# Fewer, wider TensorE products, four more staging tiles and four zero stores under way in a decode attention and GEGLU backward kernel

## The chip, the cores and the metric

The kernel runs on one core of a Trainium2 chip. The metric is device microseconds (us) for one execution of the whole program.

## The reference

The program computes a layer's forward output and its gradients with `jax.vjp`, for one new token in each of 4 batch rows (D = 512, 32 query heads, 8 key/value heads, Dh = 128, cache length 4096, F = 1792, all bfloat16):

```python
def _A_ref(x, k_cache, v_cache, wq, wo):           # attention over the last W positions
    W = min(4096, max(256, Sk // 4))               # 1024 of 4096
    q = (x @ wq).reshape(B, Sq, Hq, Dh).transpose(0, 2, 1, 3)
    k = repeat(k_cache[:, :, Sk - W:, :], 4, axis=1)
    v = repeat(v_cache[:, :, Sk - W:, :], 4, axis=1)
    p = softmax(einsum("bhqd,bhkd->bhqk", q, k) * Dh ** -0.5)
    o = einsum("bhqk,bhkd->bhqd", p, v)
    return o.transpose(0, 2, 1, 3).reshape(B, Sq, Hq * Dh) @ wo
def _B_ref(x, w_gate, w_up, w_down):
    return (gelu(x @ w_gate) * (x @ w_up)) @ w_down
xn = layernorm(x)
f = x + _A_ref(xn, k_cache, v_cache, wq, wo) + _B_ref(xn, w_gate, w_up, w_down)
out, vjp = jax.vjp(f, ...);  return (out, *vjp(grad_out))
```

Nine outputs result: the layer's output and the gradients to x, the two caches (33.6 MB each), wq, wo, w_gate, w_up and w_down. Positions before the window have a gradient of zero, so three quarters of each cache gradient are zeros that must be written.

## The kernel before

The kernel has four stages.

*FFN.* The rows are replicated so that row `Q*b + i` (Q = 32) of x and grad_out belongs to batch row b. `h_ps` holds the two hidden products, with four column groups of TensorE side by side; `dwd`, `dwu` and `dwg` are outer products that pass through PSUM banks, are copied into a staging tile `stg` ([128, 4096] bfloat16; the pool `stage` has 4) and stored. The gradient to the layer norm's output is summed in `dxf_ps` over 112 products of 128 columns.

*Preparation of attention.* `q_ps` gets the query, heads along its free dimension, from 128 products (32 heads by 4 chunks) that take 128x128 blocks of `wq_sb` as weights and 4 columns of `xnT` as the moving operand. ACT scales it into `qs`, DVE copies that into `qs2`; `spread_rows(0, get_q)` makes from these D3q, a form with 32x32 blocks turned for the scores, and `qm`, the rows that the gradient to K needs. Then eight 32x32 transposes of `wo_sb` on DVE feed the 32 products `do_ps`, from which `spread_rows(1, get_d)` makes D3d and `dm`. `rows[k]` has a copy for each of two heads of a quadrant.

*Attention*, a loop over the 4 batch rows. `scores(0, b)` and `scores(1, b)` give S and dP in the form [128, 256]: partition (quadrant c, j-octet a, row r), with 8 DVE transposes of K or V each. `softmax` gives `P_b`. `spread(P_b)` (4 DVE multiplications by `amask`) makes `spr`, the weights of `dvdk`; `turned` makes `pT`, positions on partitions, from `P_b` by 32 products with the selectors `selp`; `odq` multiplies `pT` by V (or K) in 32 products of 256 columns, one column group per quadrant, and picks the right one of two heads with masks `om` by one ACT step and one DVE step into `odt`. `dvdk` has 32 products per call (K = 32 rows, 256 columns) into 16 `kv_ps` banks, whose copies by `evac` fill two `stg` tiles; each is stored by `result`. The k = 1 half does the same for dS, with `rows[0]`, giving the gradient to K.

*The end.* The output, the gradient to x (`dxq_ps`, 128 products of 128 columns), then `dwo` and `dwq`, 8 `stg` tiles of 8 banks each.

TensorE, VectorE, ScalarE and GpSimd run their instructions in an order that the tile framework's scheduler works out from the program; the order on SyncE (SP) is the program's (`manual_schedule`). SP issues all loads and the 32 zero stores: `zeros(n, after)` takes the next n of the list, each 1.5 MB from `ztile`, and makes each wait until the `deep`-th one before it has landed; with `after` it waits also for a compute instruction. GpSimd (POOL) issues all result stores. `evac(out, in_, n)` copies a PSUM bank to SBUF on ACT or DVE, whichever has less work by a running estimate.

Lines that the prediction follows: 117 (`mm`, all matmuls), 88 and 89 (`evac` on ACT and DVE), 93 (`t32`, transposes), 106 (`store`), 512 (`spread`), 598 (`odq`'s DVE step).

Of the kernel before, what the change touches and what calls it, by code (L numbers as in the profile page):

```python
# [8 lines left out]
ACT = mybir.ActivationFunctionType  # L9
ALU = mybir.AluOpType  # L10
# [8 lines left out]
def kernel(  # L19
# [148 lines left out]
    def mask(name, n, in_):  # L168
# [9 lines left out]
    hm = mask("hm", Q, ident_f[:].rearrange("p (h d) -> p h d", d=4))  # L178
    omt = const.tile([P, NQ, 2], FP32, name="omt")
    TT(out=omt[:], in0=gmask[:].rearrange("p (c g) -> p c g", g=2), in1=bm[:].unsqueeze(2).broadcast_to([P, NQ, 2]),  # L180
       op=ALU.mult)
    om = mask("om", 2, omt[:].rearrange("p c g -> p g c"))
    oms = const.tile([P, 2], FP32, name="oms")
    TS(out=oms[:], in0=om[:], scalar1=scale, scalar2=None, op0=ALU.mult)
    gmask_b = const.tile([P, G], BF16, name="gmask_b")
    nc.vector.tensor_copy(out=gmask_b[:], in_=gmask[:])
# [4 lines left out]
    rs2_f = rs2[:].rearrange("p c a r -> p (c a r)")  # L191
    selp = const.tile([P, 4, NQ, 8], BF16, name="selp")
    for a in range(4):
        TS(out=selp[:, a], in0=rs2[:, :, 0, :], scalar1=amask[:, a:a + 1], scalar2=None, op0=ALU.mult)

# [31 lines left out]
    fo = const.tile([P, D], FP32, name="fo")  # L227
    dxf = const.tile([P, P], FP32, name="dxf")

# [24 lines left out]

    def zeros(n, after=None, deep=3):

        for _ in range(n):
            og, b, g = ztodo.pop(0)
            z = store(nc.sync, og[b, g:g + ZG, 0:K0, :].rearrange("g (m j) d -> m g (j d)", m=ZP), zsrc, "zeros",
                      ["rest"])  # L260
            if len(zdone) >= deep:
                behind(z.ins, zdone[-deep].ins)
            if after is not None:
                behind(z.ins, after.ins)
            zdone.append(z)


    if True:
# [81 lines left out]

        dxf_ps = bank("dxf_ps", "S", (P, P))
        nc.vector.memset(dxf_ps[:], 0.0)
        nm = 0
        for wi, (wsb, dh, og) in enumerate(((wu_sb, dhu, out_7), (wg_sb, dhg, out_6))):
# [13 lines left out]
            for ch in range(4):  # L368
                sc = scratch()
                n7 = FPB // 4  # L370
                t32(sc[:, 0:n7 * P].rearrange("p (k c n) -> p c k n", k=n7, c=C),
                    pairs(wsb[:])[:, :, ch * n7 * Q:(ch + 1) * n7 * Q], 896)
                sb = sc[:, 0:n7 * P].bitcast(BF16).rearrange("p (k n r) -> p k r n", k=n7, r=2)
                for k in range(n7):
                    for r in range(2):
                        c = nm % 4
                        mm(dxf_ps[Q * c:Q * c + 4 * B, :], dhs[:, ch * n7 + k, r, :], sb[:, k, r, :], nm < 4,
                           nm >= 4 * FPB - 4, (0, Q * c))
                        nm += 1
            dwg_v = og.rearrange("(p h c) f -> h p (c f)", h=2, c=2)  # L380
# [12 lines left out]
    with tc.tile_pool(name="mid", bufs=1, reuse_waits="tile") as mid:  # L393
# [4 lines left out]
        with tc.tile_pool(name="att", bufs=1, reuse_waits="tile") as att:  # L398
# [171 lines left out]
            def dvdk(k, b, sp, r_):  # L570

                og = (out_3, out_2)[k]
                stg = [stg_tile() for _ in range(2)]
                sv = [s_[:].rearrange("p (g j d) -> p j g d", g=4, j=J) for s_ in stg]
                for j in range(0, J, 2):
                    ps = [bank("kv_ps", "w", (P, 2, 2, Dh)) for _ in range(NQ)]
                    for u in range(2):
                        for c, q in enumerate(quad):
                            mm(ps[c][:, u].rearrange("p g d -> p (g d)"), sp[q, j + u].rearrange("p a m -> p (a m)"),
                               r_[q, b].rearrange("p g d -> p (g d)"), pos=(Q * c, 0))  # L580
                    for c in range(NQ):
                        evac(sv[c // 2][:, j:j + 2, (c % 2) * 2:(c % 2) * 2 + 2, :], ps[c][:], 512)
                for hf in range(2):
                    result(og[b, hf * 4:(hf + 1) * 4, K0:Sk, :].rearrange("g (m j) d -> m g (j d)", j=J),
                           stg[hf][:].rearrange("p (g e) -> p g e", g=4))

            def odq(k, b, pT):

                ps = bank("od_ps", "x", (P, 2, Dh))
                src = (v_t, k_t)[k][b]  # L590
                for j in range(J):
                    for c, q in enumerate(quad):
                        mm(ps[q].rearrange("p g d -> p (g d)"), pT[:, j, :], src[:, 2 * c:2 * c + 2, j, :],
                           j == 0, j == J - 1, (0, Q * c))
# [3 lines left out]
                done = STT(out=t_[:], in0=ps[:, 1, :], scalar=mk[:, 1:2], in1=t_[:], op0=ALU.mult, op1=ALU.add)  # L598
                if k == 0:
# [33 lines left out]
            for b in range(B):  # L633
# [6 lines left out]
                if b == B - 1:  # L640
                    zeros(3, p_done)
                    turn_wq()
                    dP = scores(1, b)
                pT = turned(P_b, 0)
                o_done = odq(0, b, pT)
# [3 lines left out]
                else:  # L649
                    zeros(2, o_done)  # L650
                dvdk(0, b, spread(P_b, 0), rows[1])
                dS_b = softmax_d(P_f, dP)
                dST = turned(dS_b, 1)
                o_done = odq(1, b, dST)
# [3 lines left out]
                elif b == B - 1:  # L658
                    zeros(2, o_done)
                dvdk(1, b, spread(dS_b, 1), rows[0])  # L660

        with tc.tile_pool(name="end", bufs=1, reuse_waits="tile") as end:
# [28 lines left out]

            dxq_ps = bank("dxq_ps", "dP", (P, P))
            nc.vector.memset(dxq_ps[:], 0.0)
            nm = 0
            for hc in range(8):
                for k in range(8):
                    for r in range(2):
                        c = nm % 4
                        mm(dxq_ps[Q * c:Q * c + 4 * B, :], dqs[:, hc * 4 + k // 2, k % 2, r, :],
                           wqT[hc].bitcast(BF16).rearrange("p c k (n r) -> p k r c n", r=2)[:, k, r], nm < 4,  # L700
                           nm >= 124, (0, Q * c))
                        nm += 1
# [3 lines left out]
            s_d = fin("s_d", (P, P))  # L706
            TT(out=s_d[:], in0=dxq_ps[:], in1=dxf[:], op=ALU.add)
            dn_ps = bank("dn_ps", "x", (B, 4, C, Q))
            for nb in range(4):
                mm(dn_ps[:, nb].rearrange("b c n -> b (c n)"), rsum_f[:, nb * B:(nb + 1) * B], s_d[:])  # L710
            dn = fin("dn")
# [39 lines left out]
            for c in range(C):  # L751
                stg = stg_tile()
                for u in range(2):
# [36 lines left out]
```

## Time and profile before

| | before |
|---|---|
| median of 3 runs | 281.53 us (280.95 to 282.53) |
| profiled execution | 283.22 us |
| its span | 281.5 us |
| mean granted TensorE clock | 0.595 |
| PE / PEld busy | 179.4 us (64%), 1733 products / 73.2 us |
| DVE / ACT / POOL busy | 167.6 us (60%) / 122.7 us (44%) / 50.0 us (18%) |
| DMA | 111.97 MB, mean 398 GB/s |
| read from and written to HBM | 30.68 MB and 81.01 MB |
| zero stores: 32 of 1.5 MB, issue to landing (median) | 20.6 us |
| 1 MB stores from `stg`: 24, issue to landing (median) | 15.4 us |

The span is the time from the first to the last event of the profile; the difference of 1.7 us to the profiled execution's time lies around it. "Busy" is time in which an engine works on an instruction; engines overlap. PE's products are recorded after pairing, so the page counts fewer of them than the program has. The page's 40 slices are 7.04 us each. The queue q1 holds SP's transfers, q0 POOL's, q8 the fetches of TensorE's instructions.

### The profile page before, as it was taken

To read this page: it belongs to the slowest core of one execution; us is meant where nothing else is said; L and a number is where in the kernel's file an instruction comes from. 1 tells how busy PE (TensorE), PEld (TensorE's weight loads), DVE (VectorE), ACT (ScalarE), POOL (GpSimd) and SP (SyncE) were. 2 spreads that over 40 slices of the span, in tenths; PEclk is the share of its full clock that TensorE was granted. 3 is DMA by queue.
4 is the path that set the end of the run, shared out by engine and by line. 5 is a ranking of instruction groups with operands and counts; after the bars stand their busy time and mean duration, and the time that the engine had idled before them with its cause. 6 is when DMAs were issued, how large, how long until landed. Compare 5 with 4: busy or idle time off the path is not lost.

```text
span 281.5 us, 4422 instructions
## 1 busy us (share of the span) xinstructions
PE 179.4 (64%) x1733; PEld 73.2 (26%) x1735; DVE 167.6 (60%) x310; ACT 122.7 (44%) x248; POOL 50.0 (18%) x121
## 2 busy tenths in 40 slices
PE   1157998878248778497774877504779996504470
PEld 0022452322122532225322243102236351000110
DVE  7879659888943437424484086996433439514470
ACT  3243775610129348292461823500851944413470
POOL 8500100294330402204020020200020020100010
PEclk9985955559755755555555575555555956555555
DMA  7999989999999999999999999999899999999773
GB/s 275 429 452 444 377 356 423 426 422 405 429 403 427 422 407 414 418 414 428 415 402 422 404 406 424 414 395 426 363 412 400 419 402 406 416 418 415 319 306 156
DMA packets 20340, 111.97 MB, mean 398 GB/s; under 512 B 1360, under 2 KB 1376, under 8 KB 14688
## 3 DMA queue, kind: packets, MB, share of 16 engines
q1 hardware_dynamic: 13944, 81.02, 70.5%
q0 software_dynamic: 6368, 30.67, 26.9%
q8 instruction: 13, 0.21, 0.3%
q14 instruction: 7, 0.06, 0.0%
q10 hardware_dynamic: 8, 0.00, 0.0%
HBM read 30.68 MB, written 81.01 MB: 397 GB/s over the span
## 4 chain that ended last, share of the span: by engine, by line
PE 21%; issue 20%; DMA 14%; DVE 12%; ACT 4%; POOL 1%; POOLq 0%; ACTq 0%
DMA out_dram<-stg 14%; PE kv_ps L117 11%; DVE scr L93 5%; PE od_ps L117 3%; ACT stg L88 2%; DVE stg L89 2%; DVE spr L512 2%; PE sc_ps L117 2%; PE ok_ps L117 1%; PE dwq_ps L117 1%; POOL out_dram L106 1%; PE es_ps L117 1%; PE nm_ps L117 1%; ACT E_f L544 1%; PE dqr_ps L117 1%
## 5 line engine op out<-in xcount | busy, mean ns | idle before, releaser
L88 ACT CAST stg<-kv_ps 128x512 bf16<-128x512 f32 x118 | 60.0, 650 | 5.7 <-PE kv_ps L117 5.6
L106 POOL DMA_DIRECT2D out_dram<-stg x30 | 19.7, 657 | 209.9 <-ACT stg L88 147.7
L117 PE MATMUL sc_ps<-scr,bd 128*32 128x256 bf16 x256 | 19.0, 389 | 24.2 <-DVE scr L93 24.2
L93 DVE STREAM_TRANSPOSE scr<-va 128x1024 uint32<-128x1024 uint32 x16 | 18.8, 1220 | 21.9 <-PE od_ps L117 21.6
L117 PE MATMUL kv_ps<-dm,spr 32*128 32x256 bf16 x128 | 26.3, 393 | 4.7 <-ACT stg L88 2.6
L117 PE MATMUL kv_ps<-qm,spr 32*128 32x256 bf16 x128 | 24.3, 372 | 3.9 <-ACT stg L88 2.4
L117 PEld LDWEIGHTS <-spr 32*128 32x128 bf16 x256 | 11.6, 101 | 43.0 <-issue 37.2
L117 PE MATMUL dwo_ps<-dy_b,oSP 32*128 32x512 bf16 x32 | 10.1, 549 | 12.9 <-ACT stg L88 11.9
L117 PEld LDWEIGHTS <-bd 128*32 128x32 bf16 x256 | 9.2, 117 | 33.0 <-issue 31.5
L88 ACT CAST stg<-dwo_ps 128x512 bf16<-128x512 f32 x18 | 10.0, 593 | 17.2 <-PE dwo_ps L117 9.5
L544 ACT ACTIVATE E_f<-sc_ps,negm 128x256 f32<-128x256 f32 x4 | 1.9, 474 | 33.7 <-DVE negm L541 33.7
L117 PE MATMUL dwq_ps<-dqSP,xn_b 32*128 32x512 bf16 x32 | 10.5, 588 | 8.2 <-ACT stg L88 7.7
L89 DVE CAST stg<-dwq_ps 128x512 bf16<-128x512 f32 x15 | 9.9, 689 | 8.7 <-DMA out_dram<-stg 6.5
L89 DVE CAST stg<-dwo_ps 128x512 bf16<-128x512 f32 x14 | 9.1, 680 | 9.0 <-DMA out_dram<-stg 8.4
L88 ACT CAST stg<-dwg_ps 128x448 bf16<-128x448 f32 x26 | 12.2, 555 | 4.4 <-PE dwg_ps L117 3.5
L88 ACT CAST stg<-dwq_ps 128x512 bf16<-128x512 f32 x17 | 9.5, 587 | 8.7 <-DMA out_dram<-stg 7.7
L88 ACT CAST pT<-pT_ps 128x256 bf16<-128x256 f32 x8 | 3.0, 373 | 23.7 <-PE pT_ps L117 23.7
L117 PE MATMUL do_ps<-scr,dyBD 128*128 128x512 bf16 x31 | 10.1, 461 | 2.5 <-DVE scr L93 2.1
L89 DVE CAST stg<-kv_ps 128x512 bf16<-128x512 f32 x10 | 6.5, 684 | 7.8 <-PE kv_ps L117 7.7
L117 PEld LDWEIGHTS <-pT 128*32 128x32 bf16 x256 | 9.3, 138 | 5.1 <-issue 2.3
L93 DVE STREAM_TRANSPOSE scr<-wo_sb 128x1024 uint32<-128x1024 uint32 x8 | 9.7, 1233 | 1.0 <-PE do_ps L117 0.9
L93 DVE STREAM_TRANSPOSE scr<-kb 128x1024 uint32<-128x1024 uint32 x8 | 9.3, 1216 | 1.6 <-PE sc_ps L117 1.6
(200 smaller groups left out, 320.0 us busy)
## 6 DMA issues: line engine op xcount, KB each, us to landing
out_dram<-ztile SPq DMA_DIRECT2D x32, 1536.0 KB, 20.6
out_dram<-stg POOLq DMA_DIRECT2D x24, 1024.0 KB, 15.4
va<-in_A_v_cache_dram SPq DMA_DIRECT2D x8, 1024.0 KB, 14.6
out_dram<-stg POOLq DMA_DIRECT2D x6, 896.0 KB, 10.3
wq_sb<-in_A_wq_dram SPq DMA_DIRECT2D x1, 4096.0 KB, 23.1
wo_sb<-in_A_wo_dram SPq DMA_DIRECT2D x1, 4096.0 KB, 33.9
ka<-in_A_k_cache_dram SPq DMA_DIRECT2D x4, 1024.0 KB, 24.8
kb<-in_A_k_cache_dram SPq DMA_DIRECT2D x4, 1024.0 KB, 26.9
```

What stands on the lines that cost most here:

```text
L88: return nc.scalar.copy(out=out, in_=in_)
L89: return nc.vector.tensor_copy(out=out, in_=in_)
L93: nc.vector.transpose(out=out, in_=in_)
L106: d = eng.dma_start(out=out, in_=in_, **kw)
L117: nc.tensor.matmul(out, lhsT=lhsT, rhs=rhs, start=first, stop=last, **kw)
L512: TS(out=sp[:, :, a, :], in0=src[:].rearrange("p (j m) -> p j m", j=J), scalar1=amask[:, a:a + 1], scalar2=None, op0=ALU.mult)
L544: nc.scalar.activation(out=E_f[:], in_=S, func=ACT.Exp, bias=negm[:, 0:1], scale=1.0, accum_out=es[:])
```

## The change

It has these parts:

- **Shorter PE program.** `dvdk` multiplies two quadrants at a time (K = 64, 512 columns: 16 products per call instead of 32; the rows that do not belong together are masked to zero by `pm`, so `rows[k]` has four copies instead of two, and `dm` now lies in `dyBD`'s memory). `odq` multiplies four heads at a time (16 products of 512 columns; even and odd j have column groups of their own) and picks with a mask of 4 columns: one ACT step and three DVE steps. `turned` works on `spread`'s result, with 8 products by one selector `selr` instead of 32 by `selp`. `dxf_ps` and `dxq_ps` take both values of r at once: half as many products of 256 columns, and `dn_ps` sums them by 8 instead of 4 products. The query is computed in row form, 32 products of 512 columns into two `qr_ps` banks, copied out as float32 (`q_row`), and turned by 8 products into `q_ps`.
- **Four zero stores under way**: `deep` is 4 instead of 3.
- **Four more staging tiles** `more` in the last phase's pool: `dwo`'s t = 2, 3 and `dwq`'s c = 0, 1 use them, the other four use `stg`.

The bytes loaded and stored are the same. The diff, without the changed masks at the start:

```diff
+    cm = mask("cm", 2, bm[:].rearrange("p (h c) -> p c h", c=2))
+    pm = const.tile([P, 2, 2], FP32, name="pm")
+    TT(out=pm[:], in0=cm[:].unsqueeze(2).broadcast_to([P, 2, 2]), in1=g2m[:].unsqueeze(1).broadcast_to([P, 2, 2]),
+       op=ALU.mult)
...
-    selp = const.tile([P, 4, NQ, 8], BF16, name="selp")
-    for a in range(4):
-        TS(out=selp[:, a], in0=rs2[:, :, 0, :], scalar1=amask[:, a:a + 1], scalar2=None, op0=ALU.mult)
+    selr = const.tile([P, NQ, 8], BF16, name="selr")
+    nc.vector.tensor_copy(out=selr[:], in_=rs2[:, :, 0, :])
...
-    def zeros(n, after=None, deep=3):
+    def zeros(n, after=None, deep=4):
...
-                    for r in range(2):
-                        c = nm % 4
-                        mm(dxf_ps[Q * c:Q * c + 4 * B, :], dhs[:, ch * n7 + k, r, :], sb[:, k, r, :], nm < 4,
-                           nm >= 4 * FPB - 4, (0, Q * c))
-                        nm += 1
+                    c = nm % 4
+                    mm(dxf_ps[quad[c]].rearrange("p r n -> p (r n)"), dhs[:, ch * n7 + k].rearrange("p r x -> p (r x)"),
+                       sb[:, k], nm < 4, nm >= 2 * FPB - 4, (0, Q * c))
+                    nm += 1
...
-            rows = [att.tile([P, B, 2, Dh], BF16, name=n) for n in ("qm", "dm")]
+            qm = att.tile([P, B, 4, Dh], BF16, name="qm")
+            rows = [qm[:], dyBD[:].rearrange("p n r x -> p (n r x)").rearrange("p (b g d) -> p b g d", b=B, g=4)]
...
+            q_row = scratch()[:].bitcast(FP32).rearrange("p (u i d) -> p u i d", u=2, i=4)
+            for u in range(2):
+                ps = bank("qr_ps")
+                for c in range(C):
+                    for a, q in enumerate(quad):
+                        o_ = (4 * u + a) * 512
+                        mm(ps[q, :], xnT[:, c, :], wq_sb[:, c, o_:o_ + 512], c == 0, c == C - 1, (0, Q * a))
+                evac(q_row[:, u].rearrange("p i d -> p (i d)"), ps[:], 512)
             q_ps = bank("q_ps", "x", (P, Hq, B))
-            for h in range(Hq):
-                for c in range(C):
-                    mm(q_ps[:, h, :], wq_sb[:, c, h * Dh:(h + 1) * Dh], xnT[:, c, 0:B], c == 0, c == C - 1)
+            q_v = q_ps[:].rearrange("p (u a i) b -> p u a i b", u=2, a=4)
+            rows_b = ident_f[:].rearrange("p (a r b) -> p a r b", a=4, r=8)[:, :, 0, :]
+            for u in range(2):
+                for i in range(4):
+                    mm(q_v[:, u, :, i, :], q_row[:, u, i, :], rows_b)
...
-                nc.scalar.activation(out=rows[k][:, :, 0, :], in_=ps[:], func=ACT.Copy, scale=g2m[:, 0:1])
-                TS(out=rows[k][:, :, 1, :], in0=ps[:], scalar1=g2m[:, 1:2], scalar2=None, op0=ALU.mult)
+                for g in range(4):
+                    m_ = pm[:, g // 2, g % 2:g % 2 + 1]
+                    if g % 2 == 0:
+                        nc.scalar.activation(out=rows[k][:, :, g, :], in_=ps[:], func=ACT.Copy, scale=m_)
+                    else:
+                        TS(out=rows[k][:, :, g, :], in0=ps[:], scalar1=m_, scalar2=None, op0=ALU.mult)
...
-            def turned(src, k):
+            def turned(sp, k):
...
-                    for a, q in enumerate(quad):
-                        mm(ps[q, j, :], src[:, j * Q:(j + 1) * Q], selp[:, a].rearrange("p c r -> p (c r)"), pos=(0, Q * a))
+                    mm(ps[:, j, :], sp[:, j].rearrange("p a m -> p (a m)"), selr[:].rearrange("p c r -> p (c r)"))
...
-                for j in range(0, J, 2):
-                    ps = [bank("kv_ps", "w", (P, 2, 2, Dh)) for _ in range(NQ)]
-                    for u in range(2):
-                        for c, q in enumerate(quad):
-                            mm(ps[c][:, u].rearrange("p g d -> p (g d)"), sp[q, j + u].rearrange("p a m -> p (a m)"),
-                               r_[q, b].rearrange("p g d -> p (g d)"), pos=(Q * c, 0))
-                    for c in range(NQ):
-                        evac(sv[c // 2][:, j:j + 2, (c % 2) * 2:(c % 2) * 2 + 2, :], ps[c][:], 512)
+                for j in range(J):
+                    for h in range(2):
+                        hs = slice(64 * h, 64 * h + 64)
+                        ps = bank("kv_ps", "w", (P, 4, Dh))
+                        mm(ps[:].rearrange("p g d -> p (g d)"), sp[hs, j].rearrange("p a m -> p (a m)"),
+                           r_[hs, b].rearrange("p g d -> p (g d)"), pos=(64 * h, 0))
+                        evac(sv[h][:, j, :, :], ps[:], 512)
...
-                ps = bank("od_ps", "x", (P, 2, Dh))
+                ps = bank("od_ps", "x", (P, 4, Dh))
...
-                    for c, q in enumerate(quad):
-                        mm(ps[q].rearrange("p g d -> p (g d)"), pT[:, j, :], src[:, 2 * c:2 * c + 2, j, :],
-                           j == 0, j == J - 1, (0, Q * c))
+                    for h in range(2):
+                        c = 2 * (j % 2) + h
+                        mm(ps[quad[c]].rearrange("p g d -> p (g d)"), pT[:, j, :], src[:, 4 * h:4 * h + 4, j, :],
+                           j < 2, j >= J - 2, (0, Q * c))
...
-                done = STT(out=t_[:], in0=ps[:, 1, :], scalar=mk[:, 1:2], in1=t_[:], op0=ALU.mult, op1=ALU.add)
+                for g in range(1, 4):
+                    done = STT(out=t_[:], in0=ps[:, g, :], scalar=mk[:, g:g + 1], in1=t_[:], op0=ALU.mult, op1=ALU.add)
...
-                pT = turned(P_b, 0)
+                sp = spread(P_b, 0)
+                pT = turned(sp, 0)
...
-                dvdk(0, b, spread(P_b, 0), rows[1])
+                dvdk(0, b, sp, rows[1])
...
-                dST = turned(dS_b, 1)
+                sp = spread(dS_b, 1)
+                dST = turned(sp, 1)
...
-                dvdk(1, b, spread(dS_b, 1), rows[0])
+                dvdk(1, b, sp, rows[0])
...
+            more = [end.tile([P, 4096], BF16, name=f"more{n}") for n in range(4)]
...
-                stg = stg_tile()
+                stg = stg_tile() if t < 2 else more[t - 2]
...
-                stg = stg_tile()
+                stg = more[c + 2] if c < 2 else stg_tile()
```

More of the change, by code (lines that the diff above doesn't have):

```diff
@@ L178 @@
     hm = mask("hm", Q, ident_f[:].rearrange("p (h d) -> p h d", d=4))
-    omt = const.tile([P, NQ, 2], FP32, name="omt")
-    TT(out=omt[:], in0=gmask[:].rearrange("p (c g) -> p c g", g=2), in1=bm[:].unsqueeze(2).broadcast_to([P, NQ, 2]),
+    hmask = mask("hmask", 2, bm[:].rearrange("p (j h) -> p h j", h=2))
+    omt = const.tile([P, 2, 4], FP32, name="omt")
+    TT(out=omt[:], in0=gmask[:].rearrange("p (h g) -> p h g", g=4), in1=hmask[:].unsqueeze(2).broadcast_to([P, 2, 4]),
        op=ALU.mult)
-    om = mask("om", 2, omt[:].rearrange("p c g -> p g c"))
-    oms = const.tile([P, 2], FP32, name="oms")
+    om = mask("om", 4, omt[:].rearrange("p c g -> p g c"))
+    oms = const.tile([P, 4], FP32, name="oms")
     TS(out=oms[:], in0=om[:], scalar1=scale, scalar2=None, op0=ALU.mult)
+    cm = mask("cm", 2, bm[:].rearrange("p (h c) -> p c h", c=2))
+    pm = const.tile([P, 2, 2], FP32, name="pm")
+    TT(out=pm[:], in0=cm[:].unsqueeze(2).broadcast_to([P, 2, 2]), in1=g2m[:].unsqueeze(1).broadcast_to([P, 2, 2]),
+       op=ALU.mult)
     gmask_b = const.tile([P, G], BF16, name="gmask_b")
@@ L227 @@
     fo = const.tile([P, D], FP32, name="fo")
-    dxf = const.tile([P, P], FP32, name="dxf")
+    dxf = const.tile([P, 2, P], FP32, name="dxf")
     wq_sb = wres.tile([P, C, HD], BF16, name="wq_sb")
@@ L349 @@
             result(dwd_v[h], stg[:, 0:FB // 2 * D])
-        dxf_ps = bank("dxf_ps", "S", (P, P))
+        dxf_ps = bank("dxf_ps", "S", (P, 2, P))
         nc.vector.memset(dxf_ps[:], 0.0)
@@ L690 @@
             TT(out=out_b[:], in0=out_ps[:], in1=x_b[0:B, :], op=ALU.add)
-            dxq_ps = bank("dxq_ps", "dP", (P, P))
+            dxq_ps = bank("dxq_ps", "dP", (P, 2, P))
             nc.vector.memset(dxq_ps[:], 0.0)
@@ L696 @@
                 for k in range(8):
[L697 to L702, printed above, removed]
+                    c = nm % 4
+                    mm(dxq_ps[quad[c]].rearrange("p r n -> p (r n)"),
+                       dqs[:, hc * 4 + k // 2, k % 2].rearrange("p r x -> p (r x)"),
+                       wqT[hc].bitcast(BF16).rearrange("p c k (n r) -> p k r c n", r=2)[:, k], nm < 4,
+                       nm >= 60, (0, Q * c))
+                    nm += 1
             xn4 = fin("xn4")
             TS(out=xn4[:], in0=x_b[0:B, :], scalar1=mv[0:B, 0:1], scalar2=rstd[0:B, 0:1], op0=ALU.subtract, op1=ALU.mult)
-            s_d = fin("s_d", (P, P))
+            s_d = fin("s_d", (P, 2, P))
             TT(out=s_d[:], in0=dxq_ps[:], in1=dxf[:], op=ALU.add)
@@ L709 @@
             for nb in range(4):
-                mm(dn_ps[:, nb].rearrange("b c n -> b (c n)"), rsum_f[:, nb * B:(nb + 1) * B], s_d[:])
+                for r in range(2):
+                    mm(dn_ps[:, nb].rearrange("b c n -> b (c n)"), rsum_f[:, 16 * r + nb * B:16 * r + (nb + 1) * B],
+                       s_d[:, r], r == 0, r == 1)
             dn = fin("dn")
```

## The prediction

> **What bounds the kernel now.** I read the page's DMA lines first, since a program that moves 112 MB may be paced by its transfers.
>
> ```profile
> DMA  7999989999999999999999999999899999999773
> ...
> q1 hardware_dynamic: 13944, 81.02, 70.5%
> q0 software_dynamic: 6368, 30.67, 26.9%
> q8 instruction: 13, 0.21, 0.3%
> ```
>
> The DMA engines are busy in nearly all 40 slices; q1 (SP's loads and zero stores) and q0 (POOL's result stores) fill 97.4% of the span between them. PE is busy 64% and DVE 60%, so neither can be the bound over the whole. What a change can win lies where the engines idle. The stretches (us; busy time of PE, PEld, DVE, ACT, POOL; clock; DMA share; GB/s) show where:
>
> ```profile
> 202.00:204.00 2.00, 2.00 (x9) 0.41 (x8) 0.00 (x0) 2.00 (x6) 0.00 (x0) 0.50 0.48 203
> 204.00:260.00 56.00, 37.71 (x395) 15.44 (x394) 25.60 (x53) 24.45 (x50) 5.17 (x8) 0.59 1.01 411
> 260.00:265.00 5.00, 1.43 (x6) 0.40 (x4) 2.01 (x4) 1.16 (x3) 0.53 (x1) 0.50 0.94 387
> 265.00:270.00 5.00, 4.33 (x15) 1.07 (x15) 3.94 (x7) 4.34 (x9) 0.53 (x1) 0.50 0.42 174
> 270.00:275.00 5.00, 2.70 (x8) 0.36 (x5) 3.00 (x5) 2.68 (x5) 1.06 (x2) 0.50 0.86 352
> 275.00:282.00 7.00, 0.00 (x0) 0.00 (x0) 0.00 (x0) 0.00 (x0) 0.00 (x0) 0.50 0.38 154
> ```
>
> There is a hole of 1.0 us at 202 to 204, and in the last phase 0.3 + 2.9 + 0.7 us before 275. Who waits there is in the waits and in POOL's timeline:
>
> ```profile
> ACT stg L88 <- DMA out_dram<-stg: 15.4, 4, 6.7
> DVE stg L89 <- DMA out_dram<-stg: 14.9, 4, 7.1
> ```
>
> ```profile
> 268.02 0.53 POOL L106 DMA_DIRECT2D out_dram<-stg  x1 [5.28 <-ACT stg L88]
> 270.92 0.53 POOL L106 DMA_DIRECT2D out_dram<-stg  x1 [2.37 <-DVE stg L89]
> 274.15 0.53 POOL L106 DMA_DIRECT2D out_dram<-stg  x1 [2.69 <-issue]
> ```
>
> The evacuations of `dwo` and `dwq` wait for a staging tile to be stored; the last three stores are then issued 2.9 and 3.2 us apart, while 1 MB takes 2.5 us.
>
> One reading stands against an easy gain. Each transfer leaves sixteen completion marks in the trace's DMA records, one per DMA engine. Of the last zero store (issued at 247.13) fifteen marks lie between 258.95 and 260.20 and one at 264.74: one engine runs 5 us behind. The last marks of the last six result stores are 267.03, 269.55, 272.05, 274.56, 277.00 and 279.45, always 2.4 to 2.5 us apart. That engine has no idle time in the tail; only the other fifteen have. Its lag was 1.4 us at 88, 3.5 at 116, 2.4 at 124, 5.1 at 152, 8 to 9 from 170 to 195 and 5.0 at 241.
>
> **The change part by part.**
>
> *Shorter PE program.* The orders of the two programs have 3342 and 2015 PE instructions. The 13 fetches on q8 come every 249 PE instructions (346 issued at the first, 3338 at the thirteenth), so 8 are left. Each takes 0.88 to 1.03 us on one DMA engine, and the packet behind it is stretched by 0.3 (441 ns where its like takes 159): 1.3 us. Five fewer are 6.5 us on sixteen engines, 0.4 us each if they spread (the first three lie on three different engines, by how packets follow one another), 1.3 if the last engine loses one of its own. The Trainium skill (Runtime: NRT & Kernel Launch, Instruction fetch mechanics) has programs fetched in 16 KiB blocks of 256 instructions, with the cost mostly hidden; the block agrees with q8's bytes, and by that rule this term would be nothing.
>
> *The query.* These rows price it (ns min/median/max, first and last start):
>
> ```profile
> L117 PE MATMUL q_ps<-xnT,wq_sb x128: 164/166/188, 33.3 to 40.6; 128*128 128x4 bf16 x128
> L117 PE MATMUL h_ps<-wg_sb,xnT x16: 552/581/581, 13.1 to 14.2; 128*32 128x448 bf16 x16
> ```
>
> 128 narrow products, 4.7 us of PE between 33 and 41 while ACT waits 2.6 us for `dwg`, go: the FFN ends 2.5 us earlier. In their place come 32 wide products at the end of the FFN. `h_ps` starts 16 in 1.1 us at clock 1.0, so 0.15 us each at 0.5: 4.7 us (9.6 if they pack as `dwq_ps` does, 0.3 each), of which 1.2 fit in PE's gaps. An evacuation (0.65) and 8 fp32 products (0.33 each, as the `ok_ps` group: 2.7) follow, then ACT's scaling and DVE's copy (0.9), and on DVE all transposes of `wo_sb` now queue behind that copy. They start at 57.6 - 2.5 + 3.5 + 4.2, less the 1.7 that D3q and its wait took ahead of them: about 61, 3.5 late. Two more row writes on DVE (0.71 each) make it 5. Ends: 1 (the FFN gains all 4.7) and 11 (0.3 us products, no gaps used). What hides it is zero stores: fast engines have them until 98.5, and the first `dvdk` store, at 92.65 with 1.5 us to its first packet, has 4.3 us of room; the lagging engine has 3 more. Cost: 0.5 us on fifteen engines, 0 on the last.
>
> *Turning and output of attention.*
>
> ```profile
> L512 DVE TENSOR_SCALAR spr<-P_b,amask x16: 277/283/287, 83.8 to 198.5; 128x256 bf16<-128x256 bf16 x16
> L598 DVE SCALAR_TENSOR_TENSOR odt<-od_ps,om,odt x4: 307/308/309, 96.6 to 210.7; 128x128 f32<-128x128 f32 x4
> ```
>
> `turned` now waits for all of `spread` (0.88 us a set, where its 32 products had run beside it in 0.41); behind it on PE stand the `kv_ps` products and for those ACT. 8 products take 0.1, so the queue is 0.1 to 0.9 late, I take 0.3 because `kv_ps` waited for `spr` before too. `odq` gains two DVE steps, 0.6 to 0.7. The wider `kv_ps`, `od_ps`, `dxf` and `dxq` products stream as many columns and fill as many banks; ACT sets their pace at 0.5 us a bank, from 85.4 to 93.3 for 16. So 1 us per half at most, 8 us over the loop, at no cost while engines have queued work: with 5 from before, `dwo` starts at 243 instead of 230.
>
> *Four zero stores.* SP waits 73 us for zero stores. The zero store of 202.81 waited for the last mark of the one issued at 179.39; with four it goes out after 188.5. Every load keeps the same bytes ahead of it in SP's queue, so it lands no later; q1 and q0 never both run out. Gain: the 1.0 us hole, on fifteen engines.
>
> *Four more tiles.* `dwo` and `dwq` no longer wait for stores: eight tiles at 2.9 us (their rate from 268 on) end at 243 + 23 = 266, against 271 when the fast engines need the last one. The fifteen close 0.5 + 3.1 + 0.5 + 0.7 = 4.8 us (gaps between median marks, over 2.45 each). If that cover were gone, each us `dwq` is late beyond 271 costs one.
>
> **The sum.** Fifteen engines: 278.2 - 4.8 - 1.0 - 0.4 + 0.5 = 272.5. The end is the sixteenth: 272.5 plus its lag. Whether lag carries over is not shown; its ends are 0 and the 6.5 which leave 279. I take 4, the middle of its history between 116 and 241 outside the peak (2.4 to 5.1, nearest the tail's 5.0): 276.5 against 279.45, a gain of 2.9. The profiled execution took 283.22 for a span of 281.5; 283.22 - 2.9 = 280.3, and the runs' median lies 1.69 below it: **278.6**.
>
> **Rivals.**
> 1. *The lag stays.* The lagging engine is busy to the end, its bytes are the same, and it gains its share of fetches alone, 0.4 to 1.3: 281.1 to 280.2. For it: the even 2.45 us steps, and lag that grew from 88 on, where the `dvdk` stores run, which stay. Against: the lag rose and fell by several us within the run. The Trainium skill (DMA: Bandwidth & Descriptors, Latency and other measured facts) has engines 7 and 15 as usually slower, perhaps from the descriptor rings of GpSimd's queue; this speaks against the change, and the marks agree that one engine lags, but do not name it. 0.23.
> 2. *The query's detour drains the queues.* If the first scores come 11 instead of 5 us late, and the loop's first half adds 1, the first store starts at 106 where zero stores ended at 98.5: 7.7 us without work on fifteen engines, 4.7 on the last. Less the 0.4 of fetches the end is 283.8 on the last engine: 285.9 in the runs. It turns slower by 0.5% from a delay of about 9 us. For it: DVE's in-order queue puts 8 transposes of 1.23 us behind the query. Against: the `h_ps` rate and 2.5 us freed earlier. 0.28.
> 3. *The program is shorter, but PE was never the bound, and the tail stays gated*, because the new tiles lie where attention's tiles lay and wait for their readers. The last reader of those is done by 227, 15 us ahead: 281 to 282. 0.03.
>
> My forecast has 0.46. About 0.5%, 1.4 us, is what a measurement of this kernel can tell from no change. Faster by more takes the forecast's 0.46; rival 1 and rival 3 give 0.26 within it, rival 2 and its milder forms 0.28 slower. The range runs from 276.0 (lag 1.4, its value at 88) to 284.5: it takes in rivals 1 and 3 and the milder third of rival 2, and leaves out the rest of it. The forecast's own range is 276.0 to 280.1.
>
> **What would show it.** Right: q8 with 8 fetches; no ACT or DVE wait on stores of `stg` worth 15 us; a DMA share near 1 from 260 to the end; last marks at 2.5 us steps ending some 3 us earlier. The first scores after 76 and before 80 show the query's price. Wrong: the last six last marks unchanged though the median marks move forward by 5 (rival 1), or a DMA share well under 1 between 96 and 106 (rival 2).

## The result, and the profile after

| | before | after |
|---|---|---|
| median of the runs made together | 281.70 us (280.95 to 282.53, 4 runs) | 286.91 us (285.00 to 287.75, 4 runs) |
| ratio | | 1.0162, 95% interval 1.0126 to 1.0198 |
| profiled execution, its span | 283.22, 281.5 us | 285.00, 283.3 us |
| first result store of attention issued | 92.65 us | 99.15 us |
| last result store of attention issued | 227.45 us | 243.58 us |
| last `dwq` store issued, last landing | 274.15, 279.45 us | 275.49, 281.25 us |

The kernel became 5 us slower; 3 us faster was forecast, with a range up to 284.5 us. The two traces hold only 1.8 us of the difference (spans of 281.5 and 283.3): the profiled execution of the changed kernel was the fastest of its four, that of the kernel before lay 1.5 us above its median. The page of the changed kernel, with the DMA engines' slices, their queues, and the shares by engine of the chain that ended last:

```profile
DMA  7999989999999889999999999999969999998995
...
q1 hardware_dynamic: 13944, 81.02, 69.8%
q0 software_dynamic: 6368, 30.67, 27.1%
q8 instruction: 8, 0.13, 0.2%
...
PE 33%; DVE 21%; issue 8%; ACT 8%; POOLq 0%; ACTq 0%; DVEq 0%
```

The 8 fetches are as forecast. The tail is no longer the 7, 7, 3 of before, but two new dips ("holes" below) stand at slices 14 to 15 and 30 (counted from 1), and no transfer is left in the chain that ended last: it goes through PE, DVE and ACT alone. The stretches of the changed kernel (us; busy time of PE, PEld, DVE, ACT, POOL; clock; DMA share; GB/s):

```profile
98.00:104.00 6.00, 3.55 (x49) 1.56 (x48) 3.56 (x7) 1.71 (x4) 2.38 (x6) 0.75 0.65 240
...
202.00:212.00 10.00, 4.02 (x37) 2.05 (x36) 6.62 (x13) 1.35 (x4) 0.00 (x0) 0.50 0.82 345
212.00:217.00 5.00, 4.07 (x18) 1.18 (x19) 2.91 (x6) 3.84 (x10) 0.00 (x0) 0.50 0.77 319
217.00:230.00 13.00, 10.77 (x81) 4.86 (x83) 5.07 (x13) 4.96 (x11) 1.50 (x2) 0.50 1.00 394
230.00:260.00 30.00, 22.44 (x178) 7.44 (x171) 18.76 (x40) 17.38 (x35) 2.61 (x4) 0.78 0.95 390
260.00:275.00 15.00, 12.29 (x39) 2.88 (x38) 12.15 (x19) 11.89 (x22) 2.66 (x5) 0.50 1.02 423
```

2.1 us are empty at 98 to 104 (0.35 of 6), 1.8 + 1.2 at 202 to 217, 1.5 at 230 to 260. At 202 to 217 all ungated zeros (those that wait for no compute) are gone: SP's next zero stores wait for the last softmax and go out from 212.15 on. The waits for staging tiles have shrunk from 15.4 and 14.9 us to the last two rows here, and both of these lie in the FFN, before 60 us; none is left in the tail. Two waits stand in the loop: `turned`'s for `spread` is new, DVE's for the first step of `odt` was 8.1 us (us in total, times, longest):

```profile
PE pT_ps L117 <- DVE spr L530: 12.1, 7, 1.8
DVE odt L616 <- ACT odt L614: 11.6, 3, 4.2
DVE stg L89 <- DMA out_dram<-stg: 3.9, 1, 3.9
ACT stg L88 <- DMA out_dram<-stg: 3.6, 1, 3.6
```

POOL's timeline in the tail (start, us, what, idle time before and what ended it) and the new products and steps (ns min/median/max, first and last start):

```profile
254.12 0.55 POOL L106 DMA_DIRECT2D out_dram<-stg  x1 [9.80 <-ACT stg L88]
257.64 0.55 POOL L106 DMA_DIRECT2D out_dram<-stg  x1 [2.96 <-ACT more L88]
...
275.49 0.53 POOL L106 DMA_DIRECT2D out_dram<-stg  x1 [2.61 <-issue]
```

```profile
L117 PE MATMUL qr_ps<-wq_sb,xnT x32: 487/632/634, 52.2 to 56.5; 128*32 128x512 bf16 x32
L616 DVE SCALAR_TENSOR_TENSOR odt<-od_ps,om,odt x12: 309/346/351, 102.6 to 226.0; 128x128 f32<-128x128 f32 x12
```

The stores of the tail are issued 2.6 to 4.1 us apart because ACT and DVE fill the tiles at that pace; POOL waits for them, not for transfers. The last two tiles' sixteen completion marks lie within 1.1 us of each other (277.74 to 278.80, 280.28 to 281.25). Before, the last mark of a transfer came up to 9 us behind the median of its sixteen; here each hole let the late engines catch up (all marks of a transfer within 0.3 us at 103 and 0.2 at 217).

### The profile page after: what moved, and what is told of

It reads as the page before. It is cut to its first block, busy times and chain, and to the rows that moved or that the text cites. A ratio compares the mean times of both kernels' runs of the same rounds, so it can differ in the third digit from the quotient of the medians.

```text
span 283.3 us, 3158 instructions
## 1 busy us (share of the span) xinstructions
PE 178.3 (63%) x1095; PEld 65.1 (23%) x1095; DVE 176.2 (62%) x329; ACT 124.7 (44%) x251; POOL 49.9 (18%) x121
## 4 chain that ended last, share of the span: by engine, by line
PE 33%; DVE 21%; issue 8%; ACT 8%; POOLq 0%; ACTq 0%; DVEq 0%
PE kv_ps L117 13%; DVE scr L93 7%; PE od_ps L117 5%; ACT stg L88 4%; PE ok_ps L117 3%; ACT more L88 2%; DVE dqs L631 2%; PE sc_ps L117 2%; PE dwo_ps L117 2%; DVE spr L530 2%; PE dwq_ps L117 2%; DVE stg L89 1%; PE dxq_ps L117 1%; DVE wq_sb L93 1%; DVE wq_t L93 1%
## 5 line engine op out<-in xcount | busy, mean ns | idle before, releaser
L106 POOL DMA_DIRECT2D out_dram<-stg x26 | 17.5, 676 | 194.8 <-ACT stg L88 157.7
L117 PE MATMUL kv_ps<-dyBD,spr 64*128 64x512 bf16 x64 | 27.5, 591 | 1.0 <-ACT stg L88 1.0
L117 PE MATMUL kv_ps<-qm,spr 64*128 64x512 bf16 x64 | 20.7, 486 | 5.4 <-ACT stg L88 3.1
L117 PEld LDWEIGHTS <-spr 64*128 64x128 bf16 (+1 forms) x192 | 11.8, 104 | 46.1 <-issue 30.6
L616 DVE SCALAR_TENSOR_TENSOR odt<-od_ps,oms,odt 128x128 f32<-128x128 f32 x12 | 4.1, 345 | 11.8 <-ACT odt L614 11.6
L117 PE MATMUL pT_ps<-selr,spr 128*128 128x32 bf16 x64 | 3.2, 190 | 12.1 <-DVE spr L530 12.1
L93 DVE STREAM_TRANSPOSE scr<-ka 128x1024 uint32<-128x1024 uint32 x8 | 9.5, 1220 | 1.1 <-PE r_ps L117 1.0
L117 PEld LDWEIGHTS <-xn_b 32*128 32x128 bf16 x64 | 5.2, 108 | 20.4 <-issue 20.4
L507 POOL COPY bd<-D3d 32x64 bf16<-32x64 bf16 x32 | 6.8, 229 | 16.0 <-DVE D3d L93 11.0
L117 PE MATMUL ok_ps<-odt,selh 128*128 128x32 f32 x32 | 7.2, 387 | 3.2 <-DVE odt L616 3.2
## 6 DMA issues: line engine op xcount, KB each, us to landing
out_dram<-stg POOLq DMA_DIRECT2D x20, 1024.0 KB, 10.2
```

The source lines that it names most:

```text
L93: nc.vector.transpose(out=out, in_=in_)
L106: d = eng.dma_start(out=out, in_=in_, **kw)
L117: nc.tensor.matmul(out, lhsT=lhsT, rhs=rhs, start=first, stop=last, **kw)
L507: nc.gpsimd.tensor_copy(out=t_[q, :, :, g2, :, o_:o_ + 4], in_=src[q, b, g2])
L616: done = STT(out=t_[:], in0=ps[:, g, :], scalar=mk[:, g:g + 1], in1=t_[:], op0=ALU.mult, op1=ALU.add)
```

## The experiments

Two theories came first. Theory A: compute comes late and the transfers run dry; of that, A1 says that the tail then follows compute, A2 that the transfers still set the end and only holes lengthen it. Theory B: four zero stores at once use up the zeros, and that is the loss. "Landing" is the last completion mark in the profiled execution, "the slow engine" whichever DMA engine gives a transfer's last mark; the marks do not name it, so that it is the same one throughout is not shown. All ratios are to the kernel before on the same chip, with 95% intervals. In the code cuts, a line in brackets stands for the row form of the query, as the change shows it.

### Undoing one part, or doing one alone

**after_old_query**: the changed kernel with

```diff
-            (qr_ps, q_row, q_v: row form)
+            for h in range(Hq):
+                for c in range(C):
+                    mm(q_ps[:, h, :], wq_sb[:, c, h * Dh:(h + 1) * Dh], xnT[:, c, 0:B], c == 0, c == C - 1)
```

> The changed kernel with the query as before (128 narrow products in the FFN's gaps). Theory A, compute comes late and the transfers run dry: first result store of the attention loop near 93.5 instead of 99.15 us, DMA share of 98 to 104 above 0.95 instead of 0.65, every later store some 6 us earlier, the tail near 277 to 280 us in the runs, clearly below 286.9. Theory B, four zero stores at once use the zeros up too early and that is the loss: the hole near 202 to 217 stays and the time stays above 284.

Measured: 0.9946 (0.9926 to 0.9966), faster than before. First store 93.54, last `dwq` store 271.86, landing 276.60. Its stretches:

```profile
98.00:104.00 6.00, 3.77 (x25) 2.77 (x29) 2.24 (x10) 0.88 (x3) 0.74 (x4) 0.50 1.01 407
202.00:217.00 15.00, 10.93 (x57) 3.65 (x57) 4.88 (x12) 9.84 (x22) 0.81 (x2) 0.50 0.86 357
```

The early hole is gone, the one behind the last batch row stays, as theory B has it, yet the ratio falls from 1.0162 to 0.9946, 6 us, with four zero stores at once. Theory B falls.

**query_alone**: the kernel before with the row form.

```diff
-            for h in range(Hq):
-                for c in range(C):
-                    mm(q_ps[:, h, :], ...)
+            (qr_ps, q_row, q_v: row form)
```

> The kernel before with the query in row form alone. Theory A: first store near 98.5, a hole of about 2 us at 98 to 104, dwo starts 6 us late but its stores are held by staging tiles as before; 283 to 284.5 us, a ratio of 1.005 to 1.01. If the query's detour is hidden: 281 to 282. Theory B: no loss.

Measured: 1.0023 (1.0005 to 1.0041), 0.7 us, less than theory A expected. Stores come 5 us late (97.79 for 92.65), but the landing was 278.29: the same edit costs 6 us in one kernel and under 1 in the other. Its price is not in the edit but in what lies behind it.

**tiles_alone**: the kernel before with the four `more` tiles.

```diff
-                stg = stg_tile()
+                stg = stg_tile() if t < 2 else more[t - 2]
...
-                stg = stg_tile()
+                stg = more[c + 2] if c < 2 else stg_tile()
```

> The kernel before with four more staging tiles alone. The prediction's step (fifteen DMA engines' idle time in the tail comes back, less the lag): 278 to 279.5. The lagging-engine theory: fifteen engines finish up to 4.8 us earlier, the last one ends where it did: 281 to 281.7, last landing marks of the last six stores still 2.5 us apart and one engine about 5 us behind.

Measured: 0.9993 (0.9966 to 1.0021), no difference. The last stretches:

```profile
260.00:265.00 5.00, 0.85 (x2) 0.00 (x0) 1.20 (x2) 0.89 (x2) 0.53 (x1) 0.50 1.01 414
265.00:270.00 5.00, 0.00 (x0) 0.00 (x0) 0.00 (x0) 0.00 (x0) 0.00 (x0) 0.50 1.01 421
270.00:275.00 5.00, 0.00 (x0) 0.00 (x0) 0.00 (x0) 0.00 (x0) 0.00 (x0) 0.50 0.56 233
275.00:281.00 6.00, 0.00 (x0) 0.00 (x0) 0.00 (x0) 0.00 (x0) 0.00 (x0) 0.50 0.04 15
```

The last store goes out at 262.27 instead of 274.15 and the queues stay full to 270. Of its sixteen marks fifteen lie between 272.34 and 274.09, one at 278.94. A DMA share of 0.04, which is less than one engine of sixteen (0.06), is what the last 6 us consist of. This is one lagging engine by itself: 12 us of earlier compute bring nothing.

**deep_alone**: one edit in the kernel before.

```diff
-    def zeros(n, after=None, deep=3):
+    def zeros(n, after=None, deep=4):
```

> The kernel before with four zero stores under way alone. Prediction: the 1 us hole at 202 to 204 goes, 280.5 to 281.7. Theory B: loads and result stores share with one more zero store, compute comes later or zeros run out before the last batch row: 283 or more, with a hole near 200 to 215.

Measured: 1.0010 (0.9992 to 1.0028). The hole at 202 is gone, landing 279.55; of the transfers that landed at 220, 242 and 246 the last mark came 11 to 12 us after the first and 7 to 8 after the fifteenth, so here one engine is far behind.

### What sets the changed kernel's end

**two_zeros_less**: the changed kernel with two zero stores left out.

```diff
-                    zeros(3, p_done)
+                    zeros(1, p_done)
```

> The changed kernel without two of its 32 zero stores (two of those behind the last softmax; 3 MB of the cache gradients are not written, 7.2 us of transfers at 420 GB/s). Theory A1: last dwq store still issued near 275.5, last landing near 279.5, some 1.5 us saved. Theory A2, transfers set the end: 4 us or more saved, with the last store issued earlier too.

Measured: 1.0155 (1.0123 to 1.0187), as the changed kernel, with 3 MB less to move (this part of the gradient is not written). Neither A2's 4 us nor the 1.5 of A1 were saved. Last store at 278.79 in this execution, the slowest of its six (its first store came 1 us later than in the changed kernel's, its last 3), landing 284.23:

```profile
212.00:217.00 5.00, 2.47 (x16) 1.21 (x17) 3.71 (x8) 2.90 (x8) 0.00 (x0) 0.50 0.36 148
217.00:230.00 13.00, 10.78 (x67) 4.05 (x65) 3.75 (x8) 7.14 (x15) 1.50 (x2) 0.50 0.57 217
...
278.79 0.53 POOL L106 DMA_DIRECT2D out_dram<-stg  x1 [2.61 <-issue]
```

The two stores' time became idle time of the engines. The end is compute's.

**early_zeros**: the changed kernel with two zero stores moved.

```diff
-            zeros(4)
+            zeros(6)
...
-                    zeros(3, p_done)
+                    zeros(1, p_done)
```

> The changed kernel with two zero stores moved: six instead of four at the start of attention, one instead of three behind the last softmax. Theory A1, in the tail the stores follow the end of compute: the hole at 98 to 104 closes, the one near 202 to 217 grows, the last dwq store is still issued near 275.5 and the last landing is at 279.5 to 281, so 0 to 1.5 us better than the changed kernel. Theory A2, the tail is full of transfers and only holes lengthen it: as much is saved as the holes shrink in sum, 2 us or more.

Measured: 1.0110 (1.0075 to 1.0144), 1.5 us better than the changed kernel, with overlapping intervals. In the profiled execution, the slowest of six, the last store went out at 278.35 and landed at 283.70. The slices at 93 to 107 are full, the three at 207 to 229 fell to 345, 281 and 224 GB/s. Filling a hole moves it.

### The loop

**odq_old**: as after_old_query, and `odq` as before.

```diff
-                for g in range(1, 4):
-                    done = STT(out=t_[:], in0=ps[:, g, :], scalar=mk[:, g:g + 1], in1=t_[:], op0=ALU.mult, op1=ALU.add)
+                done = STT(out=t_[:], in0=ps[:, 1, :], scalar=mk[:, 1:2], in1=t_[:], op0=ALU.mult, op1=ALU.add)
...
```

> The changed kernel with the query as before and odq as before (32 products of 256 columns, one DVE step instead of three). If the two added DVE steps lie on the path from odt to dS: dS's spread comes 1.3 us a batch row earlier than with the query alone undone, the last dwq store near 267 instead of 271.9, last landing 273 to 276; the runs 278 to 280. If they are hidden: 280.6 as with the query alone undone. If the slowest DMA engine sets the end by then: last landing near 277 to 278 with a lag of 4 us or more.

Measured: 0.9930 (0.9905 to 0.9954). Last store 263.78, as the first case expected but earlier; landing 276.48, 7.0 us behind the first mark and 12.7 behind the issue, so no longer compute's end. It is not one engine's either: the fifteenth mark came at 276.07. Beside after_old_query (0.9946) the gain is not clear of noise: with the query in time, a last store 8 us earlier brings nothing.

**wide_dvdk_only**: the kernel before, with the wide `dvdk`, the tiles and `deep=4`.

```diff
...
+                        mm(ps[:].rearrange("p g d -> p (g d)"), sp[hs, j].rearrange("p a m -> p (a m)"),
+                           r_[hs, b].rearrange("p g d -> p (g d)"), pos=(64 * h, 0))
...
```

> The kernel before with the wide dvdk, four more tiles and four zero stores (query, turned, odq, dxf and dxq as before; 12 instruction fetches). Compute is as early as before: last dwq store near 262, no hole. The lagging-engine theory: fifteen engines done near 272, the last at 278 to 279 with a lag of 5 us or more; 280 to 281.7 in the runs. If the slow engine is relieved by anything in the wide dvdk, it ends at 277 or earlier.

Measured: 1.0031 (1.0019 to 1.0044). The median, 283.28 us, lies above the 280 to 281.7 expected. Last store 256.84, the earliest of all; landing 278.61, 9.1 behind the first mark and 4.3 behind the fifteenth.

**loop_old**: the changed kernel with `turned`, `odq`, `dxf` and `dxq` as before; late query, wide `dvdk`, tiles and `deep=4` stay.

```diff
-                sp = spread(P_b, 0)
-                pT = turned(sp, 0)
+                pT = turned(P_b, 0)
...
```

> The changed kernel with turned, odq, dxf and dxq as before; the late query, the wide dvdk, the tiles and four zero stores stay. Compute theory: first result store late as in the changed kernel (98 to 99.5), but each batch row some 2.7 us faster, so the last dwq store goes out near 263 to 266, 10 us before the changed kernel's; then the slow DMA engine sets the end at 277 to 279.5 with a lag of 4 us or more, 280 to 282.5 in the runs. If the loop's lateness were not the cause, 285 or more.

Measured: 1.0028 (1.0000 to 1.0055), a median of 283.17 us, 0.7 above the range expected. First store 99.13, last 263.10, landing 278.50:

```profile
98.00:104.00 6.00, 4.53 (x72) 3.11 (x72) 3.06 (x6) 1.69 (x4) 2.56 (x8) 0.78 0.66 244
202.00:217.00 15.00, 11.56 (x119) 4.65 (x118) 6.44 (x13) 9.58 (x20) 1.50 (x2) 0.61 1.01 427
```

The early hole is as large as in the changed kernel (0.66 against 0.65), and beside wide_dvdk_only, which hasn't the late query, nothing is lost: in the hole the marks drew together, from 2.1 us apart at 99 to 0.3 at 103, where wide_dvdk_only has 3.5. So an early hole of 2 us is free here, and the loop is the other half of the loss. Each half alone costs nothing clear of noise: the late query with the old loop (loop_old beside wide_dvdk_only), the new loop with the early query (after_old_query). Only both together push compute's end well past 276 to 279 us, where the DMA engines are done in any case.

From the first store of the loop to the first of its last pair, with seven `turned` and eight `odq` between them: 133.1 us before, 130.2 in wide_dvdk_only (93.20 to 223.41), 136.3 in odq_old, 143.7 in after_old_query, 143.3 in the changed kernel. The new `turned` (with the wider `dxf` and `dxq`, which lie outside this stretch) adds 6.1, and 5.6 in turned_tiles below (93.46 to 232.15), so 0.8 to 0.9 a half; the new `odq` 7.4, 0.9 a half; the wide `dvdk` takes off 2.9. Executions of the same loop differ by 1 to 2 us.

**odq_deep3**: odq_old with three zero stores under way.

```diff
-    def zeros(n, after=None, deep=4):
+    def zeros(n, after=None, deep=3):
```

> The changed kernel with query and odq as before and three zero stores under way instead of four. If four under way feed the slow engine's lag (11 us at most in the kernel before with four, 9 with three): lag about 2 us smaller, 278 to 280 in the runs. If the slow engine's whole work is the same: 280.3 within 0.7, and a hole where a zero store waits for its last mark.

Measured: 0.9918 (0.9890 to 0.9946), landing 276.29 against 276.48. How many zero stores are under way changes nothing here.

**early_rows**: odq_old with the row form, its block moved ahead of `dxf_ps`.

```diff
+        (q_row, qr_ps, q_ps: row form)
         dxf_ps = bank("dxf_ps", "S", (P, 2, P))
```

> The changed kernel with odq as before and the query's row form computed earlier (32 wide products, two evacuations and 8 products emitted before dxf's, so that they run among the FFN's products, near 33 to 40). If the loss came from where the products lie on the path and not from the products themselves: first result store at 93 to 95, as with the query as before; 279.5 to 281 in the runs, last landing with the lag of the slow engine. If the row form itself costs: first store at 97 or later.

Measured: 0.9918 (0.9887 to 0.9950), with odq_deep3 the best version, faster than both kernels. First store 94.05.

```profile
L117 PE MATMUL qr_ps<-wq_sb,xnT x32: 376/379/389, 31.0 to 32.5; 128*32 128x512 bf16 x32
```

The 32 products that took from 52.2 to 56.5 behind the FFN, among those of `dxf_ps`, take 1.5 us at 31. A part is the clock (1.00 at 31 to 33, 0.53 at 52 to 57; 379 ns a product against 632). Not the products but their place put them on the path.

### The slow engine and the fetches

**act_queue**: odq_old with the result stores on ACT's queue.

```diff
-        return store(nc.gpsimd, out, in_, "rest", ["zeros", "rest"], single_packet=True)
+        return store(nc.scalar, out, in_, "rest", ["zeros", "rest"])
```

> The changed kernel with query and odq as before and all result stores issued by ACT on its hardware queue instead of by POOL on its software queue. If the lag of one DMA engine comes from POOL's queue: lag under 2 us through the loop, last landing near 270 to 273 (where the other fifteen were done with POOL's queue: 269.5), 273 to 276 in the runs. If the lag has another cause: it stays at 5 us or more and the time at 280, or longer by what ACT loses to issuing.

Measured: 1.0821 (1.0770 to 1.0872). With the queue, `single_packet=True` went and the order on the engines changed: DVE has the four transposes of `va` ahead of `spread` (89.32). The first result store came at 101.50, the DMA engines stood still from 92 to then (a share of 0.01 at 92 to 99), and dips follow:

```profile
DMA  7999999999980599999998999996996993999997
```

The marks of a transfer stayed within 2.4 us from 110 on, but the holes alone may have kept them there. The run decides nothing on POOL's queue.

**padded**, **padded_wide**: odq_old with products that add zero in `scores`, 384 tiny ones (13 fetches instead of 10) or 72 wide ones (11 fetches).

```diff
+                        for _ in range(16 if g2 + e else 0):
+                            mm(ps[quad[0], 0:1], ztile[quad[0], 0:Q], sb[quad[0], 0, 0, 0:1], False, False, (0, 0))
```

> The changed kernel with query and odq as before (2462 PE instructions, 10 fetches, slow engine's last landing at 276.5, 280.3 in the runs) with 384 tiny products that add zero to the scores: 3230 PE instructions, 12 or 13 fetches, the transfers the same. Fetch theory: each added fetch takes the slow engine some 0.8 us, last landing 278.5 to 279.5, 282 to 283 in the runs, beside the other kernels with 12 and 13 fetches. If something else of the change relieved the slow engine: 280.3 within 0.7.

> Control for the padded kernel: 72 products of 256 columns that add zero, about the same PE time in the same places, but 2606 PE instructions, 10 or 11 fetches. Fetch theory: 280.3 within 0.7. If it is PE's lost time that counts: as slow as the padded kernel.

Measured: 1.0011 (0.9987 to 1.0036) and 0.9973 (0.9952 to 0.9993), against 0.9930 without. Compute came 5 us later in both (last stores 268.73 and 269.40), so they compare with each other: two more fetches, 0.38%, 1.1 us, with intervals that just overlap and landings 0.5 us apart (277.19 and 276.74).

**turned_tiles**: the kernel before with the new `turned`, tiles and `deep=4` (12 fetches).

```diff
-                pT = turned(P_b, 0)
+                sp = spread(P_b, 0)
+                pT = turned(sp, 0)
```

> The kernel before with the new turned alone, four more tiles and four zero stores: 2958 PE instructions, 11 or 12 fetches. Fetch theory: between the kernels with 10 and with 13 fetches, last landing 277.5 to 278.5, 281 to 282.5 in the runs. If turned itself (fewer weight loads from P_b) relieved the slow engine: 280 to 280.5, as the kernels that have it.

Measured: 0.9979 (0.9960 to 0.9999), landing 279.39. The new `turned` is not what lets the DMA engines end earlier.

**early_rows_deep3**: early_rows with three zero stores under way (9 fetches).

```diff
-    def zeros(n, after=None, deep=4):
+    def zeros(n, after=None, deep=3):
```

> The kernel with the row form computed early and odq as before, with three zero stores under way instead of four: 9 fetches, compute in time. Fetch theory: 279 to 280.5 in the runs, no slower than with 10 fetches and three under way (280.1). If fetches don't matter: 280 to 281.

Measured: 0.9934 (0.9911 to 0.9956).

By fetches: 13 give 0.9993, 1.0010, 1.0023 (query_alone) and 1.0011 (before: 1), 12 give 1.0031, 1.0028 and 0.9979, 11 give 0.9973, 10 give 0.9930 and 0.9918, 9 give 0.9918, 0.9934 and 0.9946 (after_old_query, where compute sets the end). That fits an estimate of 0.5 to 0.7 us a fetch at the end of the DMA engines, but three kernels with 12 differ by 0.5% among themselves, and 9 are no better than 10. Nor is it one engine that is relieved: the last three marks are 273.48, 274.34 and 278.61 in wide_dvdk_only, 273.87, 276.07 and 276.48 in odq_old, with nearly the same mean of all sixteen (271.6 and 272.0). What differs is how unevenly the engines end. Fetches are a possible part of the 2 us by which the best versions beat the kernel before; the cause stays open.

## Why the prediction was wrong, point by point

The first point rests on these rows: `dwo`'s products and the store of its first tile before, then, behind the dots, `dwo`'s first products in the chain that ended last of the changed kernel.

```profile
L117 PE MATMUL dwo_ps<-dy_b,oSP x32: 371/580/604, 230.3 to 253.6; 32*128 32x512 bf16 x32
238.39 0.55 POOL L106 DMA_DIRECT2D out_dram<-stg  x1 [10.19 <-DVE pr L725]
...
245.71 0.36 PE dwo_ps L117 x4
```

- **The step that failed: "eight tiles at 2.9 us (their rate from 268 on) end at 243 + 23 = 266, against 271 when the fast engines need the last one."** `dwo` started at 245.7, 2.7 later than put, and the eight tiles took 29.8 us, not 23. The rate was that of `dwq`'s last tiles, while the first `dwo` tile shares the engines with the outputs' chain (`dxq_ps`, `dn_ps`, `dn`): it took from 230.3 to 238.39 before, which the trace had shown, and from 245.7 to 254.12 after. The last store went out at 275.49 instead of 266, and its sixteen marks came 4.8 to 5.8 us later. The cover of 5 us did not exist; two_zeros_less shows that the end is this chain's.
- **"8 us over the loop".** The loop grew by 10.2 us. `odq`'s two DVE steps, put at 0.6 to 0.7, cost 0.9 a half. `turned`, put at 0.3 in a range of 0.1 to 0.9, cost 0.8 to 0.9: the wait for `spread` (0.88 a set) counts nearly whole. The wide `dvdk`, put at nothing, gave back 2.9.
- **The query.** Its products were sized right (0.15 us each at half clock: 52.2 to 57). The first store came 6.5 us late, 5 forecast; the 2.5 us that the FFN should have gained were 0.4 (its last store 56.85, then 56.44). The hole was 2.1 us and, as loop_old shows, free; the 6 us that the query costs in the changed kernel come from compute's late end.
- **"q1 and q0 never both run out."** They do at 98 and at 202. Compute was 11 us late by then (the pair of 181.34 was stored from 192.40 on), so the gate of the last zeros opened at 212 instead of 198, while the loads and ungated zeros were done as early as ever.
- **Four tiles.** Right in size: by themselves they were to bring the median mark to 278.2 - 4.8 = 273.4, and in tiles_alone fifteen engines were done at 272.3 to 274.1. Wrong in worth: rival 1 had it, the lag carries over whole.
- **Rival 2** had the side, the cause (late compute) and nearly the time, 285.9 against 286.9, but by another account: it priced an early hole at 7.7 us, which was 2.1 and cost nothing. Its sign, a DMA share well under 1 between 96 and 106, came (0.65 at 98 to 104); that its time came near was luck.
- **The fetches**, put at 0.4 and at most 1.3 on the last engine, may bring more: padded, with three more than odq_old, is 2.3 us slower, of which its late compute may have a part. The Trainium skill (Runtime: NRT & Kernel Launch, Instruction fetch mechanics) has their cost mostly hidden. Padded against padded_wide, 1.1 us for two fetches, speaks against that here, but weakly: the two intervals just overlap.

## What to carry to other kernels

Two ends run side by side here: that of the slowest DMA engine's work and that of compute, its last store plus some 5 us; an edit is worth what it moves the later of the two, and a delay that one kernel swallows costs another its whole length. Before a delay is called covered, add up compute's own path to the last store, with the rate of each tile from that tile's row, not from the fastest. Work for which there is idle time early should be emitted there: with the same 32 products at 52 the first store came at 99.15, at 31 at 94.05, against 93.54 and 94.19 with the narrow ones.

## What the runs showed of the hardware

Under full load the DMA engines drift apart. Before, the last of a transfer's sixteen marks came 8 to 9 us behind their median at 174 to 183; in early_rows it came up to 13.8 us behind the first (at 202). In the tail it is one engine that is late in tiles_alone (fifteen marks by 274.09, the last at 278.94), wide_dvdk_only (274.34 and 278.61) and turned_tiles (275.24 and 279.39), but several in odq_old (276.07 and 276.48, the first at 269.49) and early_rows (276.61 and 277.62, the first at 270.01). SP's waits go by a transfer's last mark (before, the zero store issued at 202.81 followed the last mark of an earlier one at 202.79), so the slowest engine sets the end (landings of 276.3 to 279.6 wherever compute is in time), and idle time of the other engines is no reserve. In a hole the marks draw together (in the changed kernel from 2.7 us apart at 100 to 0.3 at 103, from 5.2 at 212 to 0.2 at 217); that this is why an early hole cost nothing in loop_old fits, but was not tested by itself. What makes an engine slow was not found.
